# Loading a quarter of the first piece of the last values by four transfers of eight partitions each

## The chip, the cores and the metric

One core of one Trainium2 chip. The metric is the device time of one execution in microseconds (us). Every run was checked against the reference and was correct. "Span" is the length of one execution in its profile; the timed value of the same execution is 1.7 to 1.9 us above it.

## The reference

Two attention layers decode one token each for four batch entries, and their outputs stand side by side. Layer A attends to the last 2,048 of 8,192 positions with 8 key/value heads; layer B to all 8,192 positions with 32 heads. Layer B carries nearly all bytes, and its values come last:

```python
q = (x @ wq).reshape(B, Sq, H, Dh).transpose(0, 2, 1, 3)        # B = 4, Sq = 1, H = 32, Dh = 128
scores = einsum("bhqd,bhkd->bhqk", q, k_cache) * (Dh ** -0.5)   # Sk = 8192
p = softmax(scores, axis=-1)
o = einsum("bhqk,bhkd->bhqd", p, v_cache)
return o.transpose(0, 2, 1, 3).reshape(B, Sq, H * Dh) @ wo
```

## The kernel before

The work is cut into chunks of two heads of one batch entry. A chunk of values is 4 MB: 128 partitions of 32,768 B, which TensorE takes as 128 tiles of 128 x 128. SyncE issues all loads in one queue, keys and values in turn, far ahead. Each load signals a semaphore when it has landed, in 16 increments. The last chunk of values (`c == NC - 1`) is loaded in five pieces, so that TensorE can begin before all of it is there; the next-to-last (`c == NC - 2`) is one load, like all before it.

```python
LASTV = (64, 32, 16, 8, 8)
...
if kind == "v" and c == NC - 1:
    j0 = 0
    for i, n in enumerate(LASTV):
        x = slice(j0 * P, (j0 + n) * P)
        sch.add_dma("sp", lambda e, x=x: e.dma_start(dst[:, x], src[:, x]), "d_vl%d" % i, waits=waits, key=("vl", j0))
        j0 += n
    return
...
sch.add_dma("sp", lambda e: e.dma_start(dst, src), "d_h%d" % at, waits=waits, key=(kind, c))
```

TensorE's side (cut): a tile of the last chunk waits for its piece, the first tile of any other chunk for its whole load.

```python
for t in range(TG):
    j = g * TG + t
    ...
    if c == NC - 1:
        waits += [("vl", j)] if ("vl", j) in sch.tk else []
    elif j == 0:
        waits += [("v", c)]
    pe_mm(po[:, base:base + n], tile_of("v", c, j), pbt[...][...], start=j == 0, stop=j == ch["NT"] - 1, waits=waits, ...)
```

After the last tile come a division, two matmuls with the output weights, a copy and the store: 3.4 us.

## Time and profile before

| | before |
|---|---|
| time, median of 6 runs in all | 1374.58 us (1374.27 to 1375.19) |
| span of the profiled run | 1373.7 us (that execution was timed at 1375.56) |
| next-to-last values landed | 1359.09 |
| first and last piece of the last values landed | 1364.00, 1368.99 |
| the last 128 tiles | 1366.39, for 3.91 us |

The prediction below shows the page, the chain and the order of time. One more view is of use: the busy time and granted TensorE clock in three stretches (columns: stretch, its length, then busy us and number of instructions for TensorE's matmuls, its weight loads, VectorE, ScalarE, GpSimd; then the granted clock, the DMA engines' busy share and GB/s).

```profile
1355.00:1359.00 4.00, 1.88 (x44) 1.64 (x40) 1.30 (x2) 1.02 (x1) 0.00 (x0) 1.00 0.98 418
1359.14:1366.30 7.16, 7.09 (x144) 6.60 (x146) 1.58 (x7) 1.04 (x5) 0.00 (x0) 0.76 0.91 377
1366.39:1370.30 3.91, 3.91 (x129) 3.79 (x127) 0.69 (x1) 0.37 (x1) 0.00 (x0) 1.00 0.24 90
```

### The profile page before, as it was taken

Reading aid. Unit: us, or ns where it says so; the run is one execution under the profiler, and the core shown is the slowest. Engines: PE = TensorE matmul, PEld = TensorE weight load, DVE = VectorE, ACT = ScalarE, POOL = GpSimd, SP = SyncE. Lnnn points to the kernel's source line nnn. Section 1 sums busy time; section 2 is a strip of 40 time slices with the busy share of each in tenths; the row PEclk is TensorE's granted clock in tenths of the full one; section 3 lists DMA queues with packets and bytes.
Section 4 is the critical chain, followed back from the end, with each engine's and each line's share of the span. In section 5 each row is a group of like instructions: output and inputs, shape, how many; then the busy total and the mean of one; then the engine's idle time right before and its main releaser. Section 6 shows DMA issues by size and latency. Waiting matters only on the chain.

```text
span 1373.7 us, 59835 instructions
## 1 busy us (share of the span) xinstructions
PE 1184.8 (86%) x27000; PEld 1134.7 (83%) x27001; DVE 656.5 (48%) x1434; ACT 434.8 (32%) x650; POOL 7.3 (1%) x28
## 2 busy tenths in 40 slices
PE   4898899888889988888889888988888888888988
PEld 4787799888878888888889878988888888888987
DVE  1675455444444544444445444544444444444543
ACT  1553233233323332232333323332332233223332
POOL 2000000000000000000000000000000000000000
PEclk9899999999999999999999999999999999999999
DMA  9999999999999999999999999999999999999998
GB/s 401 423 424 433 426 434 426 437 429 433 429 433 429 432 429 434 428 434 428 434 428 434 429 435 431 431 431 431 431 431 432 430 432 430 432 430 432 430 427 338
DMA packets 25253, 587.53 MB, mean 428 GB/s; under 512 B 2816, under 2 KB 2832, under 8 KB 6288
## 3 DMA queue, kind: packets, MB, share of 16 engines
q1 hardware_dynamic: 25208, 587.22, 99.7%
q8 instruction: 16, 0.26, 0.1%
q14 instruction: 5, 0.04, 0.0%
q10 hardware_dynamic: 24, 0.01, 0.0%
HBM read 587.21 MB, written 0.01 MB: 427 GB/s over the span
## 4 chain that ended last, share of the span: by engine, by line
DMA 59%; PE 37%; DVE 2%; issue 1%; ACT 1%; SPq 0%; DVEq 0%
DMA kv<-in_B_k_cache_dram 54%; PE tr L406 22%; PE sc L408 9%; PE po L408 3%; DMA kv<-in_B_v_cache_dram 2%; DMA kv<-in_B_wq_dram 2%; PE fin L408 2%; DMA kv<-in_A_k_cache_dram 1%; PE ms L408 1%; DVE sA L525 1%; ACT kt L474 0%; DVE rm L534 0%; ACT pba L595 0%; DVE sA L523 0%; PE ms L406 0%
## 5 line engine op out<-in xcount | busy, mean ns | idle before, releaser
L406 PE MATMUL tr<-identb,kv 128*128 128x128 bf16 x8704 | 696.7, 230 | 138.1 <-DMA kv<-in_B_k_cache_dram 133.2
L476 DVE COPY kt<-tr 128x1024 bf16<-128x1024 bf16 x736 | 502.4, 691 | 457.7 <-PE tr L406 453.1
L406 PEld LDWEIGHTS tr<-identb,kv 128*128 128x128 bf16 x8704 | 550.9, 104 | 160.3 <-DMA kv<-in_B_k_cache_dram 91.5
L474 ACT ACTIVATE kt<-tr 128x1024 bf16<-128x1024 bf16 x352 | 359.3, 1023 | 664.9 <-PE tr L406 664.7
L408 PE MATMUL sc<-qb,kt 128*128 128x64 bf16 x8704 | 448.8, 196 | 14.5 <-ACT kt L474 12.8
L408 PEld LDWEIGHTS sc<-qb,kt 128*128 128x128 bf16 x8704 | 368.9, 101 | 25.8 <-ACT kt L474 20.2
L408 PE MATMUL po<-pbb,kv 128*128 128x64 bf16 x8320 | 285.6, 192 | 6.9 <-issue 4.9
L408 PEld LDWEIGHTS po<-pbb,kv 128*128 128x128 bf16 x8320 | 264.8, 97 | 9.3 <-issue 5.1
L575 ACT ACTIVATE pbb<-sc,negb 64x128 bf16<-64x128 f32 x128 | 51.5, 403 | 257.6 <-DVE negb L562 256.9
L539 DVE TENSOR_REDUCE rm<-sc 64x1 f32<-64x128 f32 x128 | 37.0, 289 | 58.9 <-PE sc L408 58.0
L551 DVE TENSOR_REDUCE gm<-ms 1x2 f32<-1x128 f32 (+1 forms) x72 | 20.1, 279 | 48.5 <-PE ms L406 48.5
L562 DVE COPY negb<-ms 128x1 f32<-128x1 f32 (+1 forms) x72 | 11.4, 159 | 47.1 <-PE ms L408 47.1
L408 PE MATMUL ms<-identf,gx 1*128 1x1 f32 (+1 forms) x144 | 27.4, 257 | 0.8 <-DVE zA L681 0.8
L664 DVE TENSOR_TENSOR oz<-po,rz 128x8 bf16<-128x8 f32 x33 | 5.5, 167 | 41.5 <-PE po L408 41.5
L408 PEld LDWEIGHTS ms<-identf,gx 1*128 1x128 f32 (+1 forms) x144 | 21.2, 184 | 4.8 <-DVE zA L681 0.9
L575 ACT ACTIVATION_READ_ACCUMULATOR pbb<-sc,negb 64x1 f32 x128 | 23.7, 185 | 0.0
L406 PE MATMUL ms<-identf,rm 128*1 128x128 f32 (+1 forms) x72 | 19.7, 274 | 4.1 <-DVE rm L534 4.1
L408 PE MATMUL po<-pba,kv 128*128 128x64 bf16 x512 | 20.5, 199 | 2.8 <-issue 1.5
L408 PEld LDWEIGHTS po<-pba,kv 128*128 128x128 bf16 x512 | 17.9, 102 | 5.4 <-ACT pba L595 4.2
L408 PE MATMUL fin<-wos,zB 128*4 128x512 bf16 x64 | 19.0, 378 | 0.0
L555 DVE TENSOR_SCALAR gx<-gm 1x128 f32<-1x128 f32 (+1 forms) x72 | 15.9, 221 | 2.5
L681 DVE CAST zB<-ms 64x8 bf16<-64x8 f32 x64 | 10.5, 164 | 9.4 <-PE ms L408 8.9
(61 smaller groups left out, 169.7 us busy)
## 6 DMA issues: line engine op xcount, KB each, us to landing
kv<-in_B_k_cache_dram SPq DMA_DIRECT2D x63, 4096.0 KB, 26.8
kv<-in_B_v_cache_dram SPq DMA_DIRECT2D x63, 4096.0 KB, 31.2
kv<-in_A_k_cache_dram SPq DMA_DIRECT2D x8, 2048.0 KB, 12.7
kv<-in_A_v_cache_dram SPq DMA_DIRECT2D x8, 2048.0 KB, 14.4
kv<-in_A_wq_dram SPq DMA_DIRECT2D x1, 4096.0 KB, 12.3
kv<-in_B_wq_dram SPq DMA_DIRECT2D x1, 4096.0 KB, 27.2
wor<-in_A_wo_dram SPq DMA_DIRECT2D x8, 512.0 KB, 9.1
wos<-in_B_wo_dram SPq DMA_DIRECT2D x16, 256.0 KB, 20.4
```

What stands on the lines that cost most here:

```text
L406: sch.add("pe", lambda e: e.transpose(o, l, r), waits, key)
L408: sch.add("pe", lambda e: e.matmul(o, l, r, start=start, stop=stop), waits, key)
L474: sch.add("act", lambda e: e.activation(dst, src, ACTF.Copy), waits=waits, key=("ev", s))
L476: sch.add("dve", lambda e: e.tensor_copy(dst, src), waits=waits, key=("ev", s))
L525: emit = lambda e, src=src, b=b: e.scalar_tensor_tensor(out=t, in0=src, scalar=mk[:, b:b + 1], in1=t, op0=ALU.mult, op1=ALU.add)
L539: sch.add("dve", lambda e, src=src, pp=pp: e.tensor_reduce(out=rm[pp, m, 0:1], in_=src, axis=AX.X, op=ALU.max), waits=[("S", ch["s_last"]) ...
L551: sch.add("dve", lambda e: e.tensor_reduce(out=gm[0:C, m, 0:U], in_=src, axis=AX.X, op=ALU.max), waits=[("trm", c)], key=("gmax", c))
L555: sch.add("dve", lambda e: e.tensor_scalar(out=dst, in0=gv, scalar1=-scale, scalar2=None, op0=ALU.mult), waits=[("gmax", c)], key=("gx", c))
L562: sch.add("dve", lambda e: e.tensor_copy(negb[:, m, 0:C], ms[:, col:col + C]), waits=[("bc", c)], key=("negb", c))
L575: sch.add("act", lambda e, src=src, pp=pp, n=n, u=u: e.activation(probs_of(c)[pp, :, u], src, ACTF.Exp, bias=negb[pp, m, 0:1], scale=scale ...
L664: sch.add("dve", lambda e: e.tensor_tensor(out=o, in0=i0, in1=i1, op=ALU.mult), waits=waits, key=("oT", c))
L681: sch.add("dve", lambda e, src=src, pp=pp: e.tensor_copy(z[pp, :].rearrange("p (r b) -> p r b", r=k), src), waits=[("sm", c)] + free if h ...
```

## The change

About half of the 16 DMA engines run some 3 us behind the others at the end: of the 16 increments of the next-to-last values six come at 1355.62 to 1355.95 and seven at 1358.69 to 1359.09. A transfer of eight partitions uses only eight engines: in the trace of the changed kernel the first piece's semaphore has 48 records from 1356.59 on, four times eight for the small transfers and 16 for that of 96 partitions. The small transfers take turns on the same eight: when x1_probe had queued eight of them, about eight rows were under way at a time (56.5 GB/s x 2.407 us / 16,384 B = 8.3). No trace names an engine; the texts number those eight 0 to 7 and the others 8 to 15. The change gives 32 of the 128 partitions of the first piece to four such transfers and the other 96 to one, apparently so that some engines get ten rows and the others six.

```diff
-                    sch.add_dma("sp", lambda e, x=x: e.dma_start(dst[:, x], src[:, x]), "d_vl%d" % i, waits=waits, key=("vl", j0))
+                    if i == 0:
+                        for y in [slice(96 + 8 * k, 104 + 8 * k) for k in range(4)]:
+                            sch.add_dma("sp", lambda e, x=x, y=y: e.dma_start(dst[y, x], src[y, x]), "d_vl%d" % i, waits=waits)
+                        sch.add_dma("sp", lambda e, x=x: e.dma_start(dst[0:96, x], src[0:96, x]), "d_vl%d" % i, waits=waits, key=("vl", j0))
+                    else:
+                        sch.add_dma("sp", lambda e, x=x: e.dma_start(dst[:, x], src[:, x]), "d_vl%d" % i, waits=waits, key=("vl", j0))
```

## The prediction

"Port" is the word for what four neighbouring partitions share. When the prediction was recorded, that eight neighbours fill two of them at 27.0 GB/s each was an assumption; x1_probe measured it afterwards: 56.5 and 57.0 GB/s for eight neighbouring partitions, 2.407 us a row of 16,384 B, against 0.611 us for eight partitions four apart.

Two terms of the forecast's sum are cut with what they rested on: 1 to 2 us for engines that meet at a port, and 4 to 7 us in place of 3.7 us for the 96 partitions. With them the sum was 1355.5 + 9.7 + (1 to 2), so 1366 to 1367; then 4 to 7, so 1370.5 to 1374, middle 1372.3; then 5.0, 0.25 and 3.4, a span of 1381.0 and a time of 1381.9. Without them it would come to a first piece at 1368.9 and a time of some 1378.5.

> **What bounds the kernel now.** I read the page's totals first, then the chain of work that ended last, then the order of time of the last 20 us, then the transfers' landings.
>
> The page says that the transfers bound the whole: the 16 DMA engines are busy in every slice.
>
> ```profile
> DMA  9999999999999999999999999999999999999998
> DMA packets 25253, 587.53 MB, mean 428 GB/s; under 512 B 2816, under 2 KB 2832, under 8 KB 6288
> DMA 59%; PE 37%; DVE 2%; issue 1%; ACT 1%; SPq 0%; DVEq 0%
> ```
>
> But the change touches only the last 4 MB of 587 MB, so its worth is set by the last stage, not by that share. The chain of work there (start, length, what, in us):
>
> ```profile
> 1328.78 30.31 DMA kv<-in_B_v_cache_dram
> 1359.09 0.05 issue
> 1359.14 0.65 PE po L408 x16
> ...
> 1365.75 0.81 PE tr L408 x3
> 1366.56 3.76 PE po L408 x128
> ...
> 1370.64 0.61 PE fin L408 x2
> 1371.24 0.02 issue
> 1371.27 0.68 DVE outsb L716
> ```
>
> The reader is to see that the last transfer on the chain is one issued at 1328.78. That is the load of the next-to-last values (4 MB, one transfer), not a piece of the last values. TensorE waits for it, spends 7.2 us on it and on the last softmax, then takes the last values' 128 tiles. In order of time:
>
> ```profile
> 1359.14 0.65 PE L408 MATMUL po<-pbb,kv 128*128 128x64 bf16 x16 [2.06 <-DMA kv<-in_B_v_cache_dram]
> ...
> 1366.39 3.91 PE L408 MATMUL po<-pbb,kv 128*128 128x64 bf16 x128
> 1370.64 0.59 PE L408 MATMUL fin<-wol,oz 128*4 128x512 bf16 x2 [0.33 <-DVE oz L664]
> ```
>
> 128 tiles in 3.91 us are 30.5 ns each, with no wait in brackets: no piece of the last values holds TensorE up. The semaphore records of the trace agree. The pieces (64, 32, 16, 8, 8 tiles) have landed entirely at 1364.00, 1366.48, 1367.7, 1368.36 and 1368.99; TensorE wants them at 1366.4, 1368.3, 1369.3, 1369.8 and 1370.1. The slack is 2.4, 1.9, 1.6, 1.4 and 1.1 us.
>
> The same records show what the change is after. Each transfer's 16 increments come apart: for the next-to-last values six at 1355.62 to 1355.95, two at 1356.96 and 1357.06, one at 1357.48, seven at 1358.69 to 1359.09. Every later piece has this shape. About half of the DMA engines run some 3 us behind. The gap grew between 30 and 180 us, when 15 packets of 16,384 B ran in queue 8 (kind "instruction"), and stayed.
>
> Last, the queue that issues:
>
> ```profile
> 1328.78 0.33 SPq L372 DMA_DIRECT2D kv<-in_B_v_cache_dram  x1
> 1329.16 6.81 SPq L363 DMA_DIRECT2D kv<-in_B_v_cache_dram  x5
> SPq L393 <- DMA kv<-in_B_k_cache_dram: 13.4, 1, 13.4
> ```
>
> The five pieces should take five times 0.43 us; the fifth alone took 4.61 us, with nine transfers unfinished ahead of it. Afterwards SyncE waits for the second half of the last keys and only then lets TensorE transpose it.
>
> [...] The trace has only 128-partition transfers on 16 engines, and the four-partition input and output, which show four late increments each. [...] The trace gives 27.0 GB/s per engine (32,768 B every 1.2135 us)[...].
>
> **The change part by part.** It replaces one transfer of 128 rows of 16,384 B by four of eight rows (partitions 96 to 127) and one of 96 rows. All bytes stay.
>
> Removed: two of eight rows on engines 8 to 15. A row takes 0.615 us there, so they are free 1.23 us sooner for all that follows. If these are the late eight, the late landings move from 1364.0 to 1362.8 and from 1368.99 to 1367.8.
>
> Added on engines 0 to 7: ten rows for eight, 1.23 us at the engines' own rate. The two slower of the early eight land piece 0 at 1361.95 + 1.23 = 1363.2, still under 1364.0. On this count the last byte lands 0.8 us sooner. As no piece is waited for, that is worth 0.0 us at the end.
>
> Cost at the ports: each small transfer puts 131,072 B through two ports. At 27.0 GB/s a port that is 2.43 us, not 0.61 us; four in a row are 9.7 us on engines 0 to 7, where two rows of the old transfer took 1.23 us. They start when those engines finish the next-to-last values, about 1355.5[...]. The small transfers are done near 1366 to 1367. The remaining 96 partitions are six rows, 3.7 us when spread well[...]. Piece 0 then lands at 1370.5 to 1374, middle 1372.3. The four smaller pieces follow 5.0 us later (1368.99 - 1364.00), so the last lands at 1377.3. TensorE then has eight tiles left (0.25 us) and the unchanged ending (1373.7 - 1370.3 = 3.4 us): span 1381.0. The timed value is 0.9 us above the span before (1374.6 against 1373.7), so 1381.9.
>
> SyncE: four more issues at 0.43 us, 1.7 us, in a queue that then has 13 us to wait. Free, unless the stall grows (below).
>
> **The rivals.** A, ports bind (the line above): about 1382, 0.65. [...] Against: no transfer of few partitions and many bytes is in this trace, and the change looks made by someone who expected balance to win.
>
> B, ports do not bind, and balance gives what the row count says: the last byte 0.8 us earlier, nothing at the end, 1374.6 give or take 0.4. Weight 0.25. For it: the slack of 1.1 to 2.4 us on every piece. A real gain would need the next-to-last values sooner, and they stand ahead of the change in the queue.
>
> C, the issuing queue becomes the wait. If the 4.61 us stall is a limit on the number of unfinished transfers (nine), four more make SyncE wait until the next-to-last values leave the first engines (1355.6) plus 0.43 us. The release of the last keys' second half goes from 1349.4 to 1356.1. TensorE reaches that point at 1350.2 and has 2.06 us idle later, so 1356.1 - 1350.2 - 2.06 = 3.8 us comes through: 1378.4. Weight 0.10. [...]
>
> **Range and chances.** I take A's middle, 1382.0. The low end, 1374.3, lets in B; the high end, 1386.5, lets in a bad spread of the 96 partitions over ports, or a TensorE clock that drops while it waits (the granted clock was 0.76 between 1359 and 1366, after the 2.06 us wait). 2% is 27.5 us, over twice anything here: slower 0.01, faster 0.003, within 0.987.
>
> **What would show it.** A: packets of 16,384 B that take 2 to 3 us in place of 0.615, piece 0 landing after 1370, and brackets "<-DMA kv<-in_B_v_cache_dram" on the last 128 tiles, in their first tiles and again at tile 64. B: all 16,384 B packets at 0.615 us, increments closer together (a spread near 1.5 us instead of 3.5), last landing near 1368.2, the final tiles still without a wait. C: an issue longer than 4.6 us after the small transfers, and a TensorE wait before the transposes of the last keys' second half. The prediction is wrong if small transfers do not slow each other; then 1374.6 is the answer. A time under 1374 would say that the last pieces were on the chain after all, which no view here shows.

## More of the kernel before

TensorE's repeated chunks run in hardware loops, which the builder finds by comparing one window of two chunks with the next; a window that differs is written out in full.

The DMA engines move 418 GB/s while TensorE waits, and the last tiles run at full clock.

## The result, and the profile after

1386.20 us, median of 6 runs (1385.28 to 1387.62), against 1374.58: 11.6 us more. The ratio is 1.0085, 95% interval 1.0072 to 1.0098, so the change is a loss of under one per cent and falls within 2%. A ratio here is the mean time of one kernel's fast runs over that of the other's of the same rounds, so it is not quite the ratio of the medians quoted.

TensorE's order of time at the end (start, length, instruction, count, and in brackets the idle time before it and what ended it):

```profile
1362.39 1.04 PE L414 MATMUL po<-pbb,kv 128*128 128x64 bf16 x16 [5.24 <-DMA kv<-in_B_v_cache_dram]
...
1374.77 6.57 PE L414 MATMUL po<-pbb,kv 128*128 128x64 bf16 x128 [4.42 <-DMA kv<-in_B_v_cache_dram]
1381.67 0.59 PE L414 MATMUL fin<-wol,oz 128*4 128x512 bf16 x2 [0.33 <-DVE oz L670]
```

The wait for the next-to-last values is 5.24 us in place of 2.06, and the last 128 tiles, which had no wait, now wait 4.42 us for the first piece. They also take 6.57 us in place of 3.91. The sum closes: the tiles start 1374.77 - 1366.39 = 8.4 us later and take 2.7 us longer, 11.0 us, and the spans differ by 1384.7 - 1373.7 = 11.0 us. The chain of work says the same: it comes from the first piece's 96-partition load, issued at 1331.18, straight into the last tiles.

```profile
1331.18 43.54 DMA kv<-in_B_v_cache_dram
1374.77 6.58 PE po L414 x128
```

The stretches of the changed kernel, with columns as above:

```profile
1355.00:1362.30 7.30, 1.95 (x47) 1.71 (x43) 1.38 (x3) 1.02 (x1) 0.00 (x0) 0.86 0.97 221
1362.39:1370.30 7.91, 7.91 (x145) 7.05 (x145) 1.58 (x7) 1.26 (x5) 0.00 (x0) 0.71 1.00 202
1370.40:1374.70 4.30, 0.00 (x0) 0.00 (x0) 0.68 (x1) 0.15 (x1) 0.00 (x0) 0.90 0.91 209
1374.77:1381.34 6.57, 6.57 (x128) 6.45 (x128) 0.00 (x0) 0.00 (x0) 0.00 (x0) 0.55 0.25 96
```

Two things stand there. From 1355 to 1374.7 the DMA engines are as busy as ever (shares 0.91 to 1.00) and move half as much, 202 to 221 GB/s. So packets take longer; no engine lacks work. And the last tiles run at a granted clock of 0.55.

The packet records show the slow stretch by kind. From about 1355.8 on, all sixteen engines are slow, also those that still carry the next-to-last values: their packets of 32,768 B take mostly 2.2 to 2.4 us in place of 1.215, and packets of 16,384 B mostly 1.05 to 1.5 us (1.24 in the mean) in place of 0.615, whether they belong to a small transfer or to the one of 96 partitions. It ends some 0.8 us after the last rows of the first piece, which end at 1373.63: from 1374.45 on a packet of 2,048 B takes 0.084 us as before.

The landings: the next-to-last values at 1362.35 (3.26 us later), the first piece at 1374.73 (10.7 us later), the last piece at 1379.48. The increments of the first piece hold one more fact. They reach 1370.76, and then only two are missing, which come at 1374.58 and 1374.73. The last six packets of 16,384 B end in pairs, at 1371.11 and 1371.21, 1372.37 and 1372.37, 1373.49 and 1373.63. So two engines are alone at the end with some four rows more than the rest. While they finish, from 1370.07 to 1373.63, the packets of 8,192 B that the others carry for the later pieces take 0.60 us in the median in place of 0.314: two engines with rows of the first piece are enough to hold the other fourteen at half rate. I come back to both.

The issuing queue (start, length, instruction, count):

```profile
1329.45 1.38 SPq L366 DMA_DIRECT2D kv<-in_B_v_cache_dram  x4
1331.18 0.32 SPq L367 DMA_DIRECT2D kv<-in_B_v_cache_dram  x1
1331.55 4.79 SPq L369 DMA_DIRECT2D kv<-in_B_v_cache_dram  x4
```

Everything is issued by 1336.3, with over nine transfers unfinished. The stall did not grow with the number of transfers, and the release of the last keys' second half came in time: no TensorE wait appears there. Rival C of the prediction is out.

### The profile page after: what moved, and what is told of

The parts are those of the page before. It is cut to its first block, busy times and chain, and to the rows that moved or that the text cites. A ratio compares the mean times of both kernels' runs of the same rounds, so it can differ in the third digit from the quotient of the medians.

```text
span 1384.7 us, 59840 instructions
## 1 busy us (share of the span) xinstructions
PE 1184.2 (86%) x27001; PEld 1133.5 (82%) x27001; DVE 656.6 (47%) x1434; ACT 435.1 (31%) x650; POOL 7.4 (1%) x28
## 4 chain that ended last, share of the span: by engine, by line
DMA 62%; PE 36%; issue 1%; DVE 1%; ACT 1%; SPq 0%; DVEq 0%
DMA kv<-in_B_k_cache_dram 53%; PE tr L412 22%; PE sc L414 9%; DMA kv<-in_B_v_cache_dram 3%; DMA kv<-in_A_k_cache_dram 3%; PE po L414 3%; DMA kv<-in_B_wq_dram 2%; PE fin L414 2%; PE ms L414 1%; ACT kt L480 0%; DVE sA L531 0%; ACT pba L601 0%; PE ms L412 0%; DVE zA L687 0%; SPq L366 0%
## 5 line engine op out<-in xcount | busy, mean ns | idle before, releaser
L414 PE MATMUL po<-pbb,kv 128*128 128x64 bf16 x8320 | 288.7, 193 | 14.6 <-DMA kv<-in_B_v_cache_dram 9.7
L414 PEld LDWEIGHTS po<-pbb,kv 128*128 128x128 bf16 x8320 | 267.8, 98 | 17.2 <-DMA kv<-in_B_v_cache_dram 10.3
```

The costliest lines, as they stand in the source:

```text
L414: sch.add("pe", lambda e: e.matmul(o, l, r, start=start, stop=stop), waits, key)
```

## The experiments

Twelve kernels ran. Three are the kernel before with loads by themselves after its output (probes); the others are whole kernels. All outputs are right.

| run | time, us (median) | before in the same rounds | ratio, 95% interval |
|---|---|---|---|
| the change | 1386.20 | 1374.58 | 1.0085 (1.0072 to 1.0098) |
| x2_two_wide | 1383.21 | 1375.37 | 1.0061 (1.0044 to 1.0078) |
| x3_own_ports | 1383.84 | 1375.37 | 1.0062 (1.0045 to 1.0079) |
| x4_split_prev | 1376.83 | 1375.37 | 1.0012 (0.9995 to 1.0029) |
| x5_quarter | 1377.44 | 1374.61 | 1.0021 (1.0004 to 1.0037) |
| x7_halves | 1383.47 | 1374.61 | 1.0063 (1.0046 to 1.0080) |
| x8_warm | 1385.35 | 1374.61 | 1.0076 (1.0059 to 1.0093) |
| x9_split_all | 1385.33 | 1374.69 | 1.0079 (1.0065 to 1.0092) |
| x11_low_quarter | 1384.78 | 1374.69 | 1.0072 (1.0056 to 1.0087) |
| x12_split_loop | 1379.00 | 1374.48 | 1.0032 (1.0018 to 1.0045) |

### x1_probe: loads by themselves

```diff
+            rows = B_v[0, 0:2].rearrange("u (pp j) d -> (u pp) (j d)", pp=P // 2)
+            def probe(i, loads):
+                for y, s in loads:
+                    e.dma_start(kv[y, s, :], rows[y, 0:8192]).then_inc(sems["d_p%d" % i], 16)
+                e.wait_ge(sems["d_p%d" % i], 16 * len(loads))
+            probe(1, [(slice(96, 104), s) for s in range(8)])
+            ... (ten series, each waited for)
```

> The kernel before, with ten loads by themselves appended after the output, each waited for before the next; rows of 16,384 B, 1 MiB per eight loads of eight rows (probes 1 to 4), 2 MiB in two loads of 128 rows (probe 0), 2 of 64 rows, 4 of 32, 2 of 96, then eight loads of eight rows followed by two of 128 (probe 8: partitions 96 to 103; probe 9: 0, 4, ... 28). Theory P (a port of four neighbouring partitions takes 27 GB/s): a row takes 0.615 us in probe 0 and in probes 2 and 3 (eight partitions on eight ports), and about 2.4 us in probes 1 and 4 (eight partitions on two ports), so about 20 us for those and 5 us for the strided ones; probe 5 at half rate (1.2 us a row). Rival H (only the half of the partitions, 0 to 63 or 64 to 127, is limited[...]): 0.615 us in all of probes 1 to 4, 1.2 us in 5 and 6. Rival N (a port never binds): 0.615 us everywhere. In probe 8, [...] what the changed kernel showed (all sixteen at half rate) would be seen as all of them slowing.

Measured, per row of 16,384 B: 128 partitions 0.611 us. Eight neighbouring partitions (96 to 103, and 0 to 7) 2.407 us, 56.5 and 57.0 GB/s: the prediction had 2.43. Eight partitions four apart 0.611 us. 64 partitions and 32 partitions 1.28 us, 200 GB/s each; 96 partitions about 1.1 us, 220 GB/s. So eight neighbouring partitions take about 28 GB/s for each four of them, and eight partitions four apart take what their engines give. That groups of four share it is seen in x10_probe3 below, where 0 to 3 took 2.5 us a row by the side of wide loads and 0 to 7 took 2.4: the second four did not slow the first. The surprise was the mixed series. Eight loads of 96 to 103 followed by two of 128 made the rows of *all sixteen* engines 3.02 us until the small loads had ended, though these wrote to only eight partitions. I had expected six engines to stay at 0.615.

### x2_two_wide: no small transfer

```diff
+                    parts = [slice(96, P), slice(0, 96)] if i == 0 else [slice(0, P)]
+                    for y in parts:
+                        sch.add_dma(... dst[y, x], src[y, x] ...)
```

> The first piece of the last values in two transfers, partitions 96 to 127 and then 0 to 95, both over all 16 engines; no transfer of eight partitions. If the narrow transfers on engines 0 to 7 are the cause, every row takes 0.615 us and the time is 1374.6 (within 0.5). If it is the crossing of rows to ports that another engine writes (theory P), 32 rows on eight ports and then 96 rows in another order cross as well: rows of 1.2 us, the first piece landing 3 to 5 us later than before, 1366 to 1369, and 1375 to 1379 in all.

The expectation missed; the time is 7.8 us over before, two thirds of the change's loss, without one small transfer. In TensorE's order of time:

```profile
1362.25 1.04 PE L411 MATMUL po<-pbb,kv 128*128 128x64 bf16 x16 [5.25 <-DMA kv<-in_B_v_cache_dram]
1371.89 2.05 PE L411 MATMUL po<-pbb,kv 128*128 128x64 bf16 x64 [1.70 <-DMA kv<-in_B_v_cache_dram]
1374.11 2.30 PE L411 MATMUL po<-pbb,kv 128*128 128x64 bf16 x56 [0.17 <-DMA kv<-in_B_v_cache_dram]
1376.63 0.41 PE L411 MATMUL po<-pbb,kv 128*128 128x64 bf16 x8 [0.22 <-DMA kv<-in_B_v_cache_dram]
```

The wait for the next-to-last values is 5.25 us, as in the change. The first piece is there at 1371.85, 2.9 us sooner than in the change; its last increments come evenly (1370.69 to 1371.85), without a straggling pair. The clock stays up in the last tiles (64 in 2.05 us), and so the last piece sets the end. The run cannot tell the 32 partitions from the 96, since both are less than the full width.

### x3_own_ports: small transfers that spread over ports

```diff
+                    parts = [slice(c, 32, 4) for c in range(4)] + [slice(32, P)] if i == 0 else [slice(0, P)]
```

> Four transfers of eight partitions, but strided (c, c+4, ... c+28 for c = 0 to 3), so that eight rows go to eight different ports[...]; then partitions 32 to 127 in one transfer. Theory P: the narrow rows take 0.615 us and the late engines' packets of the next-to-last values stay at 1.215 us, that load lands at 1359.1 as before; the 96-row transfer still collides, so the time lies between 1374.6 and 1382. Rival (transfers over eight engines disturb whatever their partitions): as the change, 1385 to 1387, the next-to-last values at 1362.

Missed as well: 1383.84. The next-to-last values landed at 1361.89 in place of the expected 1359.1, and all engines were at half rate from about 1356.1. Again two increments of the first piece came alone, at 1372.99 and 1373.11, 2.1 us after the others. With the small transfers on eight different ports (partitions four apart, 0.611 us a row in x1_probe) the loss is 8.5 us in place of 11.6, near that of x2_two_wide, which has none: what remains comes with the 96 partitions that follow. The small rows that started before 1355.7 still took 0.61 to 0.77 us. Why the half rate follows is not shown.

### x4_split_prev: the next-to-last values in two halves

```diff
+            if kind == "v" and c == NC - 2:
+                x = slice(0, NTB // 2 * P), slice(NTB // 2 * P, NTB * P)
+                ... first half on the old semaphore, second half on "d_vp"
+                elif c == NC - 2 and j == NTB // 2:
+                    waits = waits + ["vp"]
```

> The kernel before with the next-to-last values in two loads of half the columns, and nothing of the change. If that load alone sets the end (TensorE idles 2.06 us for it and no piece of the last values is waited for), TensorE starts on its first half about 2 us sooner and the end comes 1.0 to 2.0 us sooner: 1372.6 to 1373.6. If the last pieces were on the chain after all, nothing moves: 1374.6.

This was an attempt to win, from the wait of 2.06 us that the kernel before has. It missed: 1.5 us slower in the medians, with an interval that just holds 1. The wait for the next-to-last values is gone, but the added wait makes TensorE's last window differ from the others, so it left the hardware loop. Six more 16 KB packets of the instruction queue run between 1336 and 1368, and TensorE stalls for what the profile calls issue:

```profile
1344.96 0.27 PE L413 MATMUL ms<-identf,gx 1*128 1x1 f32 x2 [1.61 <-issue]
...
1351.43 0.27 PE L411 MATMUL tr<-identb,kv 128*128 128x128 bf16 x2 [0.91 <-issue]
...
1363.82 0.36 PE L413 MATMUL po<-pbb,kv 128*128 128x64 bf16 x7 [1.46 <-issue]
...
1370.02 1.78 PE L413 MATMUL po<-pbb,kv 128*128 128x64 bf16 x55 [0.91 <-issue]
```

These four stalls add up to 4.9 us, so the run does not say what the earlier start would be worth by itself.

### x5_quarter: the same small transfers, a quarter of the bytes

```diff
+                    if i == 0:
+                        q = slice(48 * P, 64 * P)
+                        parts = [(slice(0, P), slice(0, 48 * P))] + [(slice(96 + 8 * k, 104 + 8 * k), q) for k in range(4)] + [(slice(0, 96), q)]
```

> A quarter of the change's bytes with the same number of small transfers: of the first piece, tiles 0 to 47 go in one transfer of 128 partitions; only tiles 48 to 63 (rows of 4,096 B) go as four transfers of eight partitions and one of 96. Port theory (the loss is the bytes that pass while few ports take all): about a quarter of the loss, so the first piece lands at 1366 to 1367.5 in place of 1374.7 (1364.0 before), the last at 1370 to 1372, the next-to-last values are in time (1359.1), and the time is 1374.6 to 1377. Rival (each small transfer costs a fixed time, whatever its bytes): the first piece lands after 1370 and the time is 1381 or more.

1377.44, which is 0.4 us over the range that the port theory gave and 3.6 us under what a fixed cost per transfer gave. The loss is 2.8 us, 24% of the change's 11.6, for 25% of the bytes and all of the small transfers. The first piece landed at 1366.84 and the next-to-last values in time, at 1359.29. Between these two sizes the loss goes with the bytes that pass in uneven transfers, not with the number of transfers.

### x7_halves: two transfers of 64 partitions

```diff
+                    if i == 0:
+                        parts = [(slice(64, P), x), (slice(0, 64), x)]
```

> No small transfer at all: the first piece is loaded by two transfers of 64 partitions (64 to 127, then 0 to 63), each on all 16 engines. Port theory: 64 partitions went at 200 GB/s by themselves, so all 2 MB of the piece go at half rate, rows of 16,384 B at about 1.2 us, the late part of the next-to-last values is delayed by 2 to 3.5 us, the first piece lands at 1369.5 to 1372.5 and the time is 1380 to 1384. Rival (it is the eight-partition transfers that cost): rows at 0.61 us and 1374.6.

The time is as the port theory had it, 1383.47. Both landings are later than it had them: the first piece at 1373.08 (expected by 1372.5) and the next-to-last values at 1363.41, 4.3 us later than before (expected 2 to 3.5). Two halves one behind the other do not add up to the full width: while TensorE waited for the first piece, from 1371.09 to 1373.13, the DMA engines moved 242 GB/s, against 418 in the wait of the kernel before.

### x8_warm: the change, with TensorE kept busy

```diff
+        for _ in range(110):
+            pe_mm(po[:, 8:8 + NW], identb[:, :], identb[:, 0:NW])
         for g in range(chunks[NC - 1]["NG"]):
             emit_pv(NC - 1, g)
```

> The change, with 110 matmuls that nobody reads (128x64, into columns of po that are not used) between TensorE's last work before the last values and the wait for them, some 3.4 us. Clock theory (the last 128 tiles take 6.57 us in place of 3.91 because TensorE had idled for 4.4 us): they start at 1374.8 as in the change and take 3.9 to 4.9 us at a granted clock near 1; the last piece then sets the end, 1379.5 + 0.25 + 3.4 = 1383.1 of span, so about 1.5 us under the change (1384.5 against 1386.2). Rival (the tiles are slow because the transfers write to the same memory at the time): they take 6.5 us again and the time is 1386 or more.

```profile
1371.89 3.37 PE L414 MATMUL po<-identb 128*128 128x64 bf16 x110
1376.37 2.05 PE L414 MATMUL po<-pbb,kv 128*128 128x64 bf16 x64 [1.10 <-DMA kv<-in_B_v_cache_dram]
1378.60 2.31 PE L414 MATMUL po<-pbb,kv 128*128 128x64 bf16 x56 [0.19 <-DMA kv<-in_B_v_cache_dram]
1381.12 0.41 PE L414 MATMUL po<-pbb,kv 128*128 128x64 bf16 x8 [0.21 <-DMA kv<-in_B_v_cache_dram]
```

With 110 useless matmuls in the wait, the 128 tiles take 2.05 + 2.31 + 0.41 = 4.8 us, at a granted clock of 1.00, while the transfers write as before; and the last piece sets the end. In the change the end comes 1384.7 - 1379.48 = 5.2 us after the last landing, here 1384.9 - 1381.07 = 3.8 us. So in these two executions the idle time cost 1.4 us through the clock. The total fell by 0.85 us between the medians, less than the 1.5 expected, and the two kernels' times overlap (1385.06 to 1386.67, and 1385.28 to 1387.62): in the profiled run the first piece landed at 1376.32, 1.6 us later than in the change's, and nothing here says why the collisions of transfers differ that much between runs.

The clock records show when it falls. The changed kernel's clock is either 0.50 or 1.00; it falls 3.0 and 3.5 us after the last matmul ahead of the two waits and is back 4.6 and 5.9 us after the two restarts. In the traces of both kernels all changes of the clock lie on a grid of 3.41 us, and less idling than one step of it was enough: in the kernel before, the clock fell at 1359.64, after a wait of 2.06 us and 0.5 us after TensorE had gone on. After waits of 2.04 us (x7_halves) and 2.86 us (x3_own_ports) the last 128 tiles took 5.46 us (at 0.69 in x7_halves), so these two runs paid for the clock as well; after 1.70 us (x2_two_wide) the clock stayed up, at 1.00.

### x6_probe2 and x10_probe3: how many held-up engines hold the others

The same kind of series as in x1_probe; each small one of seven loads is followed by three loads of 128 partitions.

```diff
+            probe(2, [(slice(0, 2), s) for s in range(7)] + full)          # x6_probe2
+            probe(0, [(slice(0, 4), s, 1) for s in range(7)] + full)       # x10_probe3
+            probe(2, [(slice(96, 98), s, 1) for s in range(7)] + full)
+            probe(3, [(slice(96, 100), s, 1) for s in range(7)] + full)
+            ... (and seven more series in each)
```

> The kernel before, and ten series of loads by themselves after its output (rows of 16,384 B), each waited for. Theory H (an engine at a shared port waits, and with it all sixteen): (0,9) 128 partitions: 0.61 us a row. (1) partitions 0-1, seven loads: two engines on one port, 1.2 us. (2) the same, then three loads of 128: all rows 1.2 us until the small ones are done, then 0.61. (3) partitions 0,4,8,12, seven loads, then three of 128: [...] 0.61 throughout. (4) partitions 16,20,24,28, then three of 128: [...] all 1.2 us until the small ones are done. (5) partitions 0,4,8,12, four loads, then 0,4..28, six: 0.61. (6) 0,4..28, seven loads, then three of 0-95: 0.61, and 1.1 to 1.3 once both kinds run. (7) 96-103, seven, then three of 0-95: 2.4 to 3 us on all while the small ones run. (8) 96-127, four, then three of 128: 1.2, then 0.61. Theory P (only the engines on the shared port wait): in 2, 4, 7 and 8 the rows of the other engines stay at 0.61 (1.2 in 7).

> Ten more series after the output of the kernel before, to find how many held-up engines hold the others (two on one port did not: 14 others kept 0.611 us; five on each of two ports did: all sixteen at 3.02). Each small series of seven loads is followed by three of 128 partitions. (0) partitions 0-3: four engines on one port, rows of 2.4 us; the other twelve 0.61 (theory P) or 2.4 (theory H). (1) 0-7: eight engines on two ports, 2.4; others 0.61 or 2.4. (2) 96-97: two engines and the port's own, 1.8; others 0.61 or 1.8. (3) 96-99: four and the owner, 3.0; others 0.61 or 3.0. (4) partitions 0,4..28 with rows of 32,768 B, three loads, then two of 128: [...] 1.22 throughout. (5) 64,68..92 likewise: [...] 2.4 on those sixteen while both run. (6) 32-127 three times: some 1.1 us a row. (7) 0-95 three times: the same. (8) eight loads of 0,4..28 to 3,7..31, then two of 32-127, then three of 128: 0.61 at first, 1.1 in the wide ones of 96. (9) 128 partitions: 0.61.

The rows of 16,384 B while both kinds run, from the packet records. The count of engines is an estimate: the time of the rows at the port over the 0.611 us of a row by itself. Where it is one more than the small loads have there, an engine of the wide loads would be the one more:

| small loads | engines at a shared port, estimated | their rows, us | rows of the other engines, us |
|---|---|---|---|
| 0 to 1 | 2 | 1.2 to 1.3 | 0.611 |
| 96 to 97 | 3 | 2.0 | 0.765 |
| 0 to 3 | 4 | 2.5 | 2.5 |
| 96 to 99 | 5 | 3.0 | 3.0 |
| 0 to 7 | 4 at each of two | 2.4 | 2.4 |
| 96 to 103 (x1_probe) | 5 at each of two | 3.0 | 3.0 |

The stretches of x10_probe3 show it as GB/s (last column): small loads of 0 to 3 with wide ones and then wide ones alone, 96 to 97 with wide ones, 96 to 99 with wide ones.

```profile
1377.00:1387.00 10.00, 0.00 (x0) 0.00 (x0) 0.00 (x0) 0.00 (x0) 0.00 (x0) 0.50 1.02 105
1392.00:1402.00 10.00, 0.00 (x0) 0.00 (x0) 0.00 (x0) 0.00 (x0) 0.00 (x0) 0.50 0.98 418
1443.00:1451.00 8.00, 0.00 (x0) 0.00 (x0) 0.00 (x0) 0.00 (x0) 0.00 (x0) 0.50 0.99 305
1472.00:1484.00 12.00, 0.00 (x0) 0.00 (x0) 0.00 (x0) 0.00 (x0) 0.00 (x0) 0.50 1.02 87
```

One stretch of x6_probe2, with 0 to 1 and wide loads:

```profile
1399.00:1404.00 5.00, 0.00 (x0) 0.00 (x0) 0.00 (x0) 0.00 (x0) 0.00 (x0) 0.50 1.00 397
```

So neither of my two theories holds as stated. In these series two engines at one port hold nobody else (0.611 us); three slow the others a little (0.765); four and more hold all sixteen to the pace of that port (2.4 to 3.0). The count at one port is not the whole rule: at the end of the first piece of the changed kernel two engines held fourteen at half rate. And where partitions 16, 20, 24 and 28 went with wide loads, rows were mostly 1.0 to 1.25 us on all engines too. Loads of 0, 4 to 28 with rows of 32,768 B went at 1.21 to 2.4 us beside wide ones, median near 1.4, and loads of 64, 68 to 92 at 1.2 to 3.2 us, median near 2.2. Why the second are slower is not shown, as no trace names the engine that writes to a partition. Series 3 and 5 of x6_probe2 tell little: issuing a load of partitions four apart took 0.58 to 0.71 us, so the small loads were nearly done before the wide ones began. The loads of 96 partitions, 0 to 95 and 32 to 127, went at 224 and 226 GB/s, 1.1 us a row on all engines.

### x11_low_quarter: the other end of the partitions

```diff
-                        for y in [slice(96 + 8 * k, 104 + 8 * k) for k in range(4)]:
+                        for y in [slice(8 * k, 8 + 8 * k) for k in range(4)]:
-                        ... dst[0:96, x], src[0:96, x] ...
+                        ... dst[32:P, x], src[32:P, x] ...
```

> The change with the other end of the partitions: four transfers of eight of the partitions 0 to 31, then one of 32 to 127. [...] Theory P (only the engines at a shared port wait): those late engines keep 1.215 us for 32,768 B, the next-to-last values land at 1359.1 to 1359.5, TensorE waits 2.1 us for them; the first piece is as late as in the change or 1 us earlier, time 1383 to 1386. Theory H (many engines held up at a port hold all): the late engines slow down to about 2.3 us all the same, the next-to-last values land at 1361.5 to 1363, time 1384.5 to 1387.5.

```profile
1362.93 1.03 PE L414 MATMUL po<-pbb,kv 128*128 128x64 bf16 x16 [4.95 <-DMA kv<-in_B_v_cache_dram]
1374.49 6.17 PE L414 MATMUL po<-pbb,kv 128*128 128x64 bf16 x128 [4.39 <-DMA kv<-in_B_v_cache_dram]
```

The next-to-last values landed at 1362.89; in this run eight engines are late, and all eight increments came at 1361.4 or later. That is what theory H has: the late engines are slowed with the small transfers at the other end of the partitions too. Four increments of the first piece come last, from 1371.37 on; if those are late engines with ten rows, the other four late ones are among engines 8 to 15. It does not exclude theory P by itself: no trace shows which partitions the late engines write, and rows of partitions 32 to 127 may crowd the ports of the late ones too. No run here shows a difference between the two quarters of the partitions.

### x9_split_all and x12_split_loop: a try to beat both

```diff
+            if kind == "v":
+                x = slice(0, NTB // 2 * P), slice(NTB // 2 * P, NTB * P)
+                sch.add_dma(... x[0] ..., "d_h%d" % at, waits=waits, key=(kind, c))
+                sch.add_dma(... x[1] ..., "d_g%d" % at, key=("v2", c))
+                return
+                elif j == NTB // 2 and ch["ab"] == 1:
+                    waits = waits + [("v2", c)]
```

In x12_split_loop the second half counts on `"d_h%d" % (8 if at == 4 else 9)` in place of `"d_g%d" % at`.

> A try to beat both, from what binds the kernel before at its end (TensorE waits 2.06 us for the next-to-last values): every load of values of the second kind but the last is halved, each half with its semaphore, and TensorE waits for the second half at tile 64, in every chunk alike, so that its last chunks stay in the hardware loop (in the run that halved one load alone they did not). All bytes in loads of 128 partitions. If the wait is what binds: TensorE starts the next-to-last values 1.5 to 2 us sooner, then the last piece (1369.0) sets the end: 1369.0 + 0.25 + 3.4 = 1372.7 of span, 1373.5 of time, 0.8 to 1.2 us under before. Rival (the extra issues or the one window that left the loop cost more than that): 1374.6 or more.

> The last kernel's idea with its fault taken away: that one left one window of TensorE's loop unrolled, because the new semaphores counted from zero, and lost some 10 us at 150 to 210 us of its span (365 GB/s in place of 430) while TensorE waited for its instructions; in its last stage TensorE no longer waited for the next-to-last values. Here the second halves count on two semaphores that are already in use, and TensorE's loops are those of the kernel before. If that was its only fault: no TensorE wait for the next-to-last values, the last piece lands near 1369 and sets the end, 1369.0 + 0.25 + 3.4 = 1372.7 of span, 1373.4 to 1373.9 of time. Rival (the halved loads cost more in the whole stream than the 0.9 us that they save at the end): 1374.6 or more.

Both missed. In both, the wait for the next-to-last values is gone, as meant. x9_split_all lost 5 us between 180 and 210 us, where one window of TensorE's loop had been written out, and not the 10 us that the expectation of x12_split_loop puts there: by the bytes moved it is 0.2 us behind the kernel before at 180 us, 5.2 us at 210 us and 9.6 us at 1340 us, so the rest is lost slowly, as in x12_split_loop. The same stretch of before and of x9_split_all:

```profile
180.00:210.00 30.00, 29.59 (x712) 28.47 (x708) 17.45 (x36) 12.05 (x18) 0.00 (x0) 1.00 1.00 430
```

```profile
180.00:210.00 30.00, 25.55 (x631) 24.18 (x629) 13.63 (x31) 8.74 (x15) 0.00 (x0) 1.00 0.91 365
```

x12_split_loop has the loops of the kernel before and still needs 1379.00. TensorE has no wait before the next-to-last values and one before the last:

```profile
1361.12 0.64 PE L413 MATMUL po<-pbb,kv 128*128 128x64 bf16 x16
...
1368.39 2.05 PE L413 MATMUL po<-pbb,kv 128*128 128x64 bf16 x64 [1.23 <-DMA kv<-in_B_v_cache_dram]
```

Its last piece landed at 1373.36, 4.4 us later than before, since the stream is slower throughout: between 250 and 1340 us a packet of 32,768 B took 1.2175 us in the mean of the kernel before, and two of 16,384 B took 2 x 0.6148 = 1.2296 us here. An estimate from these: 12.1 ns times 8 rows times some 56 loads of values (the 7,147 packets of 32,768 B fewer, over 128) is 5.4 us, somewhat more than the 4.4 that were lost. No version that beats the kernel before was found.

## Why the prediction was right or wrong

**Ports bind: right.** The line that had 0.65 of the weight is the one that came. Packets of the first piece slowed down, the piece landed after 1370, and the last 128 tiles waited for it. Eight neighbouring partitions by themselves took 2.407 us a row against 2.43 predicted. B (0.25) is refuted by every packet after 1355.8, C (0.10) by the issuing queue.

**The size: 4.3 us short** (1386.2 against 1381.9), within the range. It comes from three terms. The last piece's landing plus 0.25 plus 3.4 would give 1383.1, 2.1 us over the predicted span of 1381.0. The real span is 1.6 us over that. The last 0.6 us is the choice of executions: the prediction's "0.9 us above the span" sets the median of the kernel before beside the span of an execution that was timed at 1375.56, 1.0 us over that median; the profiled one of the change is only 0.3 us over its own. That the range holds is in part luck: it holds by 0.3 us, and the first error below hides part of the next two. Term by term:

- *"Four in a row are 9.7 us on engines 0 to 7"*: too large. In the kernel the small rows took 1.1 to 1.5 us each, not the 2 to 3 us named as a sign. A likely reason, not shown: the engines were apart in time (the increments of the next-to-last values came from 1355.35 to 1362.35), so the rows of one moment belonged to different transfers and ports.
- *The estimate of 1 to 2 us for the next-to-last values*: too small, 3.26 us. The step assumed that a crowded port delays only who writes to it. The probes show that from four engines at a port on, all sixteen go at its pace (2.4 to 3.0 us a row in place of 0.611); x11_low_quarter, with small transfers on partitions 0 to 31, fits that.
- *"The remaining 96 partitions are six rows", put at 4 to 7 us*: a row took 1.24 us in the mean, so six take 7.4. Most of the loss does not need the eight-partition transfers: x2_two_wide has the 96 partitions behind one transfer of 32 and loses 7.8 of 11.6 us.
- *"Piece 0 then lands at 1370.5 to 1374, middle 1372.3"*: 1374.73. The step that failed is the count of rows with its "if these are the late eight". Eight engines had ten rows and eight had six, and the engines that run late are not all among those with six. Fourteen engines were done by 1370.76; two came at 1374.58 and 1374.73. Two late engines with ten rows fit: four rows more at 1.2 us are 4.8 us. The trace does not name engines, so this is worked out from pairs of packets and increments; x3_own_ports shows such a pair, x8_warm and x11_low_quarter three or four such increments, x2_two_wide, where every engine has eight rows, none.
- *"The four smaller pieces follow 5.0 us later"*: right, 4.75.
- *"TensorE then has eight tiles left (0.25 us)"*: wrong. The clock that had been named only as a risk of the high end decided the end: after 4.42 us of idling the 128 tiles took 6.57 us and finished 1.9 us after the last piece had landed. The predicted second wait at tile 64 did therefore not show; it does in x2_two_wide and x8_warm, where the clock stayed up.

**What stays open.** Why four engines at a port hold the twelve others, and two in the probes do not, while two at the end of the changed kernel do. Whether it is the port alone: in every series a row's place in DRAM moves with its partition, so no run separates the place written from the place read. And why two profiled runs with the same loads (the change and x8_warm) differ by 1.6 us in the first piece's landing.

## What to carry to other kernels

In the loads of 128 partitions each DMA engine moved 27.0 GB/s, and eight neighbouring partitions by themselves took no more than 57.0 GB/s, about two engines' worth. So giving rows of neighbouring partitions to idle engines did not speed them up, and a crowd there slowed all engines here, also those of the transfer ahead (2.2 to 2.4 us for 32,768 B in place of 1.215). Keep the bytes of a bandwidth-bound stream in transfers of all 128 partitions; here the loss grew with the bytes that were not, about 2.8 us for a half megabyte, and without any transfer of eight partitions, cut into 32 and 96 or 64 and 64, it was still 7.8 and 8.9 of the 11.6 us. Count a wait's second cost too: here TensorE fell to half clock after waits of 2.0 us and more, after one of 1.7 us not, and what had been hidden behind the transfers became the end of the chain.
